# First MLP stage: the second of seven Strassen products is itself split by Strassen and spread over three blocks

## The chip, the cores and the metric

The kernel runs on one core of one Trainium2 chip. The metric is the device time of one execution in microseconds (us). The kernel before takes 865.07 us, the median of three runs (864.66 to 865.10).

## The reference

Attention whose pairs are masked by a hash comes first; its output is the input of an MLP with a per-feature slope (PReLU). The change touches only the MLP.

```python
def _moe_ref(x, w_in, w_out, alpha):
    h = x @ w_in                                        # (3072, 512) x (512, 2048)
    g = np.maximum(h, 0.0) + alpha * np.minimum(h, 0.0)
    return (g @ w_out).astype(np.float32)               # (3072, 2048) x (2048, 512)
```

The 3072 tokens are four batches of 768. All of it is in float32.

## The kernel before

**Stages.** Attention comes first, up to the first MLP product at 312.32 us, beside which the weights are read, rounded and combined. Then comes the MLP, batch by batch: a first stage (`ff1`, x times `w_in`, then the slope) of eight blocks, and a second stage (`ff2`, g times `w_out`) of seven products. The list `blocks` has the order, and the loop over it (`for j, (b, what, n) in enumerate(blocks)`) writes out the work of all engines by hand: `do` is `keep_in_program_order`, so each engine executes its instructions in the order in which the loop names them. DMAs of the MLP are issued by SP (`nc.sync`) and partly by GpSimd (POOL).

**The first stage.** It is one 2 by 2 Strassen step: the features are halved, the tokens of a batch (768) are halved to 384, and the inner dimension (512) is halved. Seven products of half-size matrices give the four quarters of h. Block i of eight makes 128 features of each half. `Product.times` issues one product: two matmuls of 128 by 384 (one for each 128 rows of the inner half). `Product.step(n)` names the products in the order 1, 2, 5, 6, 3, 7, 4. They are summed in three PSUM accumulators, "a", "b" and "c". Products 1, 6, 7 and 4 go to "a" in turn, and ScalarE (ACT) copies it out between them (`keep`). Product 2 goes to "b", products 5 and 3 to "c". `finish` then makes a quarter: VectorE (DVE) adds what is left to be added (L975) and applies the slope with one `scalar_tensor_tensor` (L979). The quarter "11" is product 1 plus product 2. It comes from "b" alone (ACT copies it to h, L972), as "b" is filled with product 1 first.

**Batches two to four** have a second Strassen level for products 1 and 5. `unit(b, u, before)` runs at the head of each group of four blocks. Class `Inner` makes one product for all four blocks: seven inner products (`Inner.times`, L1084: two matmuls of 128 by 192) in place of the eight halves that the four blocks would have. Its result lies in `n_s[b, u, o, f]` in SBUF. Class `Rest` is then a block that lacks products 1 and 5: its `step(1)` has ACT copy the finished product 1 from SBUF to "b" and to "a" (L999), its `step(5)` copies product 5 to "c", and the matmuls of products 2, 6, 3, 7 and 4 add to that. Inner weights are made by `sum_inner` in batch two (DVE, L1051), written to DRAM by POOL (L1052) and read back by `load_inner` in batches three and four. Inner operands of x are made by `sum_inner_x` (L1062 to L1064).

**After a pair of blocks** DVE also makes four differences of quarters of g (L983), which the second stage needs as left-hand sides. In batches two to four, blocks 0 to 5, this is done for two blocks at a time, all four differences in one go, after step 4 of the odd block. Blocks 6 and 7 do it singly.

**The second stage** does the same two-level scheme: `ff2` has one product of the first level for each n, made of seven inner ones (tiles z_1a, z_1b, z_1c; the number names the product). DVE makes its operands (gs L1227, ws L1219) and adds (m L1248). The accumulators "b" and "c" are single PSUM tiles (`bufs=1`) that first and second stage share. "a" is taken from three tiles of two banks (`two_banks`).

**SP queue.** `load_w` fetches the weights of a block (tile wi, all seven weight combinations, 896 KB, three buffers), `load_inner` the inner weights, `load_w2` those of the second stage (wl, two buffers), and `turn_out` writes the output (o, two buffers, L1281), with a part of that on POOL.

Of the kernel before, what the change touches and what calls it, by code (L numbers as in the profile page):

```python
# [8 lines left out]
F32 = mybir.dt.float32  # L9
# [398 lines left out]
def fast_path(  # L408
# [69 lines left out]
    w_n_s = dram.tile([2, 2, P, 4, 2 * P], F32, name="w_n_s")  # L478
    NW = NK * NF // 2
    wmax = const.tile([P, NW], F32, name="wmax")  # L480

# [145 lines left out]
    def weight_sum(i):  # L627


        i = order[i]  # L630
        lo, hi = halves(i)
        x = wx[i]
        if i < HW:
            n, m = divmod(i, 4)
            if m == 0:
                wst[n] = pool.tile([P, NM, 4, P], F32, name=f"wsi{n}", tag="wsi")
            slot = (0, 5, 1, 2)[m]
# [13 lines left out]
        do(DVE.tensor_tensor(dst.bitcast(I32), x, r, op=ALU.add))  # L651
        return (dst if i < HW else dst[:, 0])[:, :1]
# [3 lines left out]
    def weight_group(i):  # L656

        i = order[i]
        if i >= HW:
            n, m = divmod(i - HW, 2)  # L660
            if m == 1:
                nc.sync.dma_start(w_out_r[:, :, n].rearrange("m p d -> p m d"), wst[HW + n])
            return
        n, m = divmod(i, 4)
        if m < 3:
            return
        w = wst[n]
# [10 lines left out]
        for x in ((3, 5, 2), (5, 0, 5), (4, 3, 0), (6, 1, 4)):  # L678
# [207 lines left out]
    def sum_x(b, n, engine):  # L886
# [3 lines left out]
            x_m[b, to] = mid.tile([P, 2, CW], F32, name=f"x{b}_{to}", tag=f"x{to}", bufs=1)  # L890
        do(engine.tensor_tensor(x_m[b, to], x_m[b, a], x_m[b, c], op=ALU.subtract))

    def load_w(n):

        if n < B * NI:
            w_m[n] = mid.tile([P, NM, 2, P], F32, name=f"wi{n}", tag="wi", bufs=3)
            pinned(n < 3, nc.sync.dma_start(w_m[n], w_in_s[n % NI]))

    class Product:

# [30 lines left out]
        def step(self, n):  # L931
# [30 lines left out]
            elif n == 4:  # L962
                self.times("a", 2, 6, False)
                self.finish("21", self.ps["a"], None)

    def ff1(b, i):
        whole = b == 0

        def finish(c, t, more):
            if more is None:  # L970
                h = mid.tile([P, CW], F32, name=f"h{b}_{i}", tag="h")
                do(ACT.copy(h, t))  # L972
            else:
                h = t
                do(DVE.tensor_tensor(h, t, more, op=ALU.add))  # L975

            al = alpha[:, i + NI * (c[0] == "2") :][:, :1]
            m = {"11": 0, "21": 1, "22": 2, "12": 5}[c]
            do(DVE.scalar_tensor_tensor(new_g(b, m)[:, i], h, al, h, op0=ALU.mult, op1=ALU.max))  # L979
            if c == "21" and (whole or i % 2 or i > 5):  # L980
                at = slice(i if whole or i > 5 else i - 1, i + 1)
                for to, x, y in ((3, 5, 0), (5, 2, 5), (4, 2, 3), (6, 1, 4)):
                    do(DVE.tensor_tensor(new_g(b, to)[:, at], g_m[b, x][:, at], g_m[b, y][:, at], op=ALU.subtract))  # L983

        w = w_m[b * NI + i]
        kind, seeded = (Product, ("b",) if i else ()) if whole else (Rest, ("a", "b", "c"))
        made = kind(
            f"f{b}_{i}", CW, 2, lambda m, k: w[:, m, k], lambda m, k: x_m[b, m][:, k], finish, seeded=seeded,
        )
        if not whole:  # L990
            made.p1, made.p5 = (n_s[b, i // 4, o, i % 4 // 2][:, i % 2] for o in range(2))
        return made

    class Rest(Product):
# [5 lines left out]

        def step(self, n):
            if n == 1:
                self.seed("b", self.p1)
                self.seed("a", self.p1)
            elif n == 5:
                self.seed("c", self.p5)
            elif n == 6:
                self.times("a", 4, 4, False)
                self.keep("a", "u1")
            elif n == 7:  # L1010
                self.times("a", 5, 5, False)
# [9 lines left out]
    def load_inner(b, u):  # L1021

        t = late[0].tile([P, NI, 2 * P], F32, name=f"wn{b}_{u}", tag="wl")
        blocks = t[:, :4].rearrange("p i (k f) -> p i k f", k=2)
        do(nc.sync.dma_start(blocks, w_in_s[4 * u : 4 * u + 4, :, 0].rearrange("i p k f -> p i k f")))
        if b > 1:
            do(nc.sync.dma_start(t[:, 4:], w_n_s[u, 0]))
        for m, (f, kh) in QUADS.items():
            n_w[b, u, 0, m] = blocks[:, 2 * f : 2 * f + 2, kh]
        for m in range(4):  # L1030
            n_w[b, u, 0, 3 + m] = t[:, 4 + m].rearrange("p (t f) -> p t f", t=2)
        for f in range(2):
            t = late[0].tile([P, 2, 2, P], F32, name=f"wq{b}_{u}_{f}", tag="m", bufs=3)
            do(nc.sync.dma_start(t, w_in_s[4 * u + 2 * f : 4 * u + 2 * f + 2, :, 3].rearrange("i p k f -> p i k f")))
            for m, (ff, kh) in QUADS.items():
                if ff == f:
                    n_w[b, u, 1, m] = t[:, :, kh]
        for h in range(2):
            t = late[0].tile([P, 2, 2 * P], F32, name=f"wp{b}_{u}_{h}", tag=f"ws{3 + h}", bufs=2)
            if b > 1:  # L1040
                do(nc.sync.dma_start(t, w_n_s[u, 1, :, 2 * h : 2 * h + 2]))
            for m in range(2):
                n_w[b, u, 1, 3 + 2 * h + m] = t[:, m].rearrange("p (t f) -> p t f", t=2)
            n_w[b, u, h] = t

    def sum_inner(b, u, o):

        if b != 1:
            return
        for m, x, op, y in ((3, 21, ALU.add, 2), (4, 3, ALU.subtract, 0), (5, 0, ALU.subtract, 21), (6, 1, ALU.subtract, 4)):  # L1050
            do(DVE.tensor_tensor(n_w[b, u, o, m], n_w[b, u, o, x], n_w[b, u, o, y], op=op))  # L1051
            nc.gpsimd.dma_start(w_n_s[u, o, :, m - 3].rearrange("p (t f) -> p t f", t=2), n_w[b, u, o, m])  # L1052

    def sum_inner_x(b, o):

        x = x_m[b, 3 * o]
        if o == 0:
            t = mid.tile([P, 4, HC], F32, name=f"xn{b}_0", tag="x", bufs=1)
        else:
            t = late[0].tile([P, 4, HC], F32, name=f"xn{b}_1", tag="gs5", bufs=1)  # L1060
# [6 lines left out]
    class Inner:  # L1067
# [36 lines left out]
        def step(self, n):  # L1104
# [25 lines left out]
            elif n == 4:  # L1130
                self.times("a", 2, 6, False)
                do(ACT.copy(self.to(1, 0), self.bank("a")))

    def unit(b, u, before):

        def bank(name, tag=None):
# [23 lines left out]
        now = ff1(b, 4 * u)  # L1160
        now.step(1)
        two.step(7)
        now.step(2)
        now.step(5)
        two.step(4)
        if u:
            sum_w2(b, 0, 3, 4, 6, 5)
        turn_out()
        return now

    def new_g(b, m):
# [300 lines left out]
    for j, (b, what, n) in enumerate(blocks):  # L1472
# [22 lines left out]
                sum_x(b + 1, {2: 0, 4: 1, 5: 2}[n], DVE)  # L1495
        if b and what == "1" and n == 1:
            load_inner(b, 1)
        if b and what == "1" and n in (2, 3):
            sum_inner(b, 1, n - 2)
        if 0 < n2 < 7:  # L1500
# [4 lines left out]
        if j:  # L1505
            if not (b and what == "1"):
                now.step(5)
            now.step(6)
            now.step(3)
            if n2 or b == 0:  # L1510
                sum_w2(b, n2, 6)
            if b and what == "1" and (n + 1) % 4:
                after = ff1(b, n + 1)
                after.step(1)
            now.step(7)
            if n2 or b == 0:
                sum_w2(b, n2, 5)
            sum_g2(b, n2, 5)
# [26 lines left out]
        if j + 1 < len(blocks):  # L1545
# [45 lines left out]
```

## Time and profile before

| what | value |
|---|---|
| median of three runs | 865.07 us (864.66, 865.10, 865.07) |
| the profiled execution | 865.96 us |
| its span, first to last instruction | 863.8 us |
| granted TensorE clock | 0.998 |
| POOL busy | 150.1 us (17%) |
| HBM | 169 GB/s over the span |

The six stages of batches two to four, cut by hand at the start of the first inner product, of the second stage, and so on (us of busy time in each stretch):

| stretch, us | length | PE | DVE | ACT |
|---|---|---|---|---|
| batch 2, first stage, 449.55 to 522.9 | 73.35 | 72.82 | 57.43 | 35.17 |
| batch 2, second stage, 522.9 to 585.4 | 62.50 | 61.99 | 59.75 | 10.70 |
| batch 3, first stage, 585.4 to 656.5 | 71.10 | 71.10 | 52.08 | 35.02 |
| batch 3, second stage, 656.5 to 719.0 | 62.50 | 62.50 | 59.93 | 11.03 |
| batch 4, first stage, 719.0 to 790.1 | 71.10 | 71.10 | 51.78 | 35.02 |
| batch 4, second stage, 790.1 to 853.4 | 63.30 | 62.66 | 57.41 | 11.03 |

How to read it: the profile is of one execution, and its times are counted from the first instruction. "Busy" is the time in which an engine has an instruction in work; the ends of matmuls are modelled, so what a product takes is read from the distance between starts. In timelines a line gives the start, the length, the engine, the source line, the operation, out<-in, and in brackets the idle time ahead of it with what ended it. One product of the first stage appears as four matmul records, an inner one as four shorter ones.

### The profile page before, as it was taken

The numbers are of one execution on the slowest core, as the hardware profiler recorded it, in microseconds if no ns is written. First come the engines' busy times: TensorE is split into PE (matmuls) and PEld (weight loads), VectorE is DVE, ScalarE is ACT, GpSimd is POOL, SyncE is SP. The second block draws the span as 40 slices with busy tenths as digits, with TensorE's granted clock in tenths as the row PEclk, the third lists the DMA queues.
The fourth block names the chain that finished last, engine by engine and source line by source line (L and its number), as shares of the span: only waits on it lengthen the run. The fifth ranks groups of instructions, "written<-read, shape, count | busy, mean of one in ns | idle before, by whom it ended". The sixth has DMA issues, their size and how long they took to land.

```text
span 863.8 us, 15130 instructions
## 1 busy us (share of the span) xinstructions
PE 851.8 (99%) x5602; PEld 591.1 (68%) x5602; DVE 751.6 (87%) x1210; ACT 415.9 (48%) x778; POOL 150.1 (17%) x313
## 2 busy tenths in 40 slices
PE   9999999999999999999999999999999999999996
PEld 4444444444445445569996769998668999677996
DVE  6999999999999977889996979996769997769985
ACT  7777888878788833231115541114452114453111
POOL 1322423333334310210015100003000001200001
PEclk9999999999999999999999999999999999999999
DMA  8956879879698436775344734333845334830342
GB/s 203 191 130 132 205 178 240 167 205 243 131 252 208 145 126 234 245 288 215 128 141 139 276 134 170 120 144 97 315 140 174 143 109 130 297 135 0 104 159 60
DMA packets 174659, 147.97 MB, mean 171 GB/s; under 512 B 120832, under 2 KB 155824, under 8 KB 170992
## 3 DMA queue, kind: packets, MB, share of 16 engines
q1 hardware_dynamic: 159776, 117.35, 46.7%
q0 software_dynamic: 11792, 28.24, 10.8%
q10 hardware_dynamic: 3008, 1.33, 0.6%
q8 instruction: 46, 0.75, 0.4%
q14 instruction: 37, 0.30, 0.1%
HBM read 115.35 MB, written 30.41 MB: 169 GB/s over the span
## 4 chain that ended last, share of the span: by engine, by line


## 5 line engine op out<-in xcount | busy, mean ns | idle before, releaser
L790 ACT ACTIVATE pt<-sc 128x768 f32<-128x768 f32 x192 | 153.9, 813 | 3.1 <-PE sc L787 2.8
L787 PE MATMUL sc<-qT,kT 64*128 64x384 f32 x768 | 155.2, 482 | 0.0
L820 PE MATMUL av<-pt,vn 128*32 128x385 f32 (+1 forms) x1536 | 127.0, 485 | 0.0
L820 PEld LDWEIGHTS av<-pt,vn 128*32 128x32 f32 x1536 | 50.3, 109 | 73.8 <-issue 68.8
L787 PEld LDWEIGHTS sc<-qT,kT 64*128 64x128 f32 x768 | 68.9, 187 | 37.0 <-issue 36.9
L1281 POOL DMA_DIRECT2D out_dram<-o x52 | 28.3, 552 | 349.6 <-DVE o L1274 348.8
L983 DVE TENSOR_TENSOR g<-g,g 128x384 f32<-128x384 f32 (+1 forms) x92 | 63.5, 711 | 1.6
L787 PE MATMUL sc<-qb,kb 64*128 64x384 bf16 x384 | 63.9, 323 | 0.5 <-ACT pt L790 0.3
L979 DVE SCALAR_TENSOR_TENSOR g<-h,alpha 128x384 f32<-128x384 f32 x63 | 37.8, 612 | 20.7 <-ACT h L972 20.7
L1227 DVE TENSOR_TENSOR gs<-g,gs 128x768 f32<-128x768 f32 x56 | 53.2, 951 | 1.0
L1227 DVE TENSOR_TENSOR gs<-g 128x768 f32<-128x768 f32 x56 | 53.2, 950 | 0.0
L1219 DVE TENSOR_TENSOR ws<-wl 128x512 f32<-128x512 f32 x56 | 38.4, 685 | 11.3 <-DMA wl<-w_out_s 9.7
L787 PEld LDWEIGHTS <-kb 64*128 64x128 bf16 x384 | 20.2, 94 | 33.9 <-issue 11.6
L607 ACT ACTIVATE wr<-raw 128x512 int32<-128x512 uint32 x32 | 22.1, 692 | 30.3 <-DVE wso L651 15.3
L748 POOL DMA_DIRECT2D qb<-hr x60 | 30.0, 507 | 26.4 <-ACT hr L743 26.4
L798 DVE TENSOR_TENSOR accp<-pt,pt 128x1536 f32<-128x1536 f32 x16 | 28.1, 1756 | 7.3 <-ACT pt L790 7.3
L803 DVE TENSOR_TENSOR accd<-accd,pt 128x1536 f32<-128x1536 f32 x16 | 28.1, 1758 | 1.7
L809 DVE TENSOR_TENSOR accd<-accd,accp 128x1536 f32<-128x1536 f32 x16 | 28.1, 1758 | 0.6
L806 DVE TENSOR_TENSOR accp<-accp,pt 128x1536 f32<-128x1536 f32 x16 | 28.0, 1752 | 0.0
L802 DVE TENSOR_TENSOR accd<-pt,pt 128x1536 f32<-128x1536 f32 x16 | 28.0, 1751 | 0.0
L1431 ACT ACTIVATE qT<-qT 128x768 f32<-128x768 f32 x15 | 12.7, 844 | 25.4 <-DMA kb<-hr 20.8
L1239 DVE TENSOR_TENSOR m<-m,m 128x768 f32<-128x768 f32 x24 | 22.7, 946 | 0.3
(448 smaller groups left out, 1861.0 us busy)
## 6 DMA issues: line engine op xcount, KB each, us to landing
wi<-w_in_s SPq DMA_DIRECT2D x32, 896.0 KB
wl<-w_out_s SPq DMA_DIRECT2D x16, 1024.0 KB
wl<-w_out_r SPq DMA_DIRECT2D x12, 1024.0 KB
raw<-in_moe_w_in_dram POOLq DMA_DIRECT2D x15, 512.0 KB, 4.9
raw<-in_moe_w_out_dram POOLq DMA_DIRECT2D x14, 512.0 KB, 4.6
w_in_s<-wsi SPq DMA_DIRECT2D x16, 448.0 KB
qn<-in_q_dram SPq DMA_DIRECT2D x64, 96.0 KB
vn<-in_v_dram SPq DMA_DIRECT2D x16, 384.0 KB
```

The costliest lines, as they stand in the source:

```text
L748: queue.dma_start(bits[name, pi][D * s : D * s + 2 * NB, half * CW : (half + 1) * CW], raw[c : c + 2 * NB],)
L787: do(PE.matmul(sc[:, s, :CW], what["k", pi][r, ks], what["q", pi][r, qs], start=first, stop=not first,))
L790: do(ACT.activation(pts[kc][:, g, :, :CW], sc[:, :, :CW], AF.Exp, scale=SCALE / DOWN))
L798: do(DVE.tensor_tensor(accp[pi], p(0), p(1), op=ALU.add))
L803: do(DVE.tensor_tensor(accd[pi], accd[pi], p(5), op=ALU.add))
L809: do(DVE.tensor_tensor(accd[pi], accd[pi], accp[pi], op=ALU.add))
L820: do(PE.matmul(av[pi][D * s + t : D * s + t + 32, g, :w], nat["v", pi][:, s, kc * D + t : kc * D + t + 32], pts[kc][:, g, s, :w], start=(k ...
L979: do(DVE.scalar_tensor_tensor(new_g(b, m)[:, i], h, al, h, op0=ALU.mult, op1=ALU.max))
L983: do(DVE.tensor_tensor(new_g(b, to)[:, at], g_m[b, x][:, at], g_m[b, y][:, at], op=ALU.subtract))
L1219: do(DVE.tensor_tensor(t, w2[b, n, x], w2[b, n, y], op=op))
L1227: do(DVE.tensor_tensor(t, g2[b, n, x], g2[b, n, y], op=ALU.subtract))
L1281: pinned(b + 1 < B and queue is nc.sync, queue.dma_start(out_v[b, ch * CH + c].rearrange("(w r) d -> r w d", r=32)[:, :, cols], src[32 * a ...
```

## The change

In batches two to four, product 2 is taken by a second Strassen level too. A new class `Third` makes it for four blocks at a time: seven inner products of two matmuls of 128 by 192, as `Inner` does. They are not run at the head of the group but one by one between the products of its first three blocks. The table `THIRD` holds the places: product 1 after step 3 of the first block, 2 after its step 7; 6, 5, 7 and 3 around the second block's steps 6, 4, 3 and 7; 4 after step 6 of the third. `Rest` loses step 2, its seed of "b", and the quarter "11" with its copy to h.

The quarter "11" now arises in `Third`: as each inner product is done, DVE adds it to product 1 straight into g, six additions of 128 by 384 for four blocks, and then applies the slopes in place (`slopes`, one instruction for a block). ACT copies once from "a" to "b" and keeps three sums. One of the `two_banks` tiles and then twice "b" are `Third`'s.

Moved along with it: step 6 of a block comes ahead of step 5 (it stood behind), so ACT's copy-out of "a" stands ahead of its seed of "c". The four differences of g for a pair of blocks go into a list, `g_due`, of which one is taken after each of the quarters "12" and "21" of blocks 0 to 5 (all that are due in blocks 6 and 7). The weights of a block are split into two tiles: wj (products 1, 2, 5; only batch one) and wi (the other four; 512 KB). `load_third` fetches the weights of the third product with two DMAs for four blocks, in batches three and four with four more from DRAM, and batch two makes those four on DVE and writes them on POOL (`sum_inner`). `sum_inner_x(b, 2)` adds three DVE instructions for a batch.

The diff, cut to its core:

```diff
@@ load_w
-            w_m[n] = mid.tile([P, NM, 2, P], F32, name=f"wi{n}", tag="wi", bufs=3)
-            pinned(n < 3, nc.sync.dma_start(w_m[n], w_in_s[n % NI]))
+            w_m[n] = {}
+            for name, slots in (("wj", WJ), ("wi", WI)):
+                if name == "wi" or n < NI:
...
@@ ff1
+    g_due = []
+    def sum_g(count):
+        for b, at, to, x, y in g_due[:count]:
+            do(DVE.tensor_tensor(new_g(b, to)[:, at], g_m[b, x][:, at], g_m[b, y][:, at], op=ALU.subtract))
+        del g_due[:count]
...
-                    do(DVE.tensor_tensor(new_g(b, to)[:, at], g_m[b, x][:, at], g_m[b, y][:, at], op=ALU.subtract))
+                    g_due.append((b, at, *x))
+            if whole or i > 5:
+                sum_g(len(g_due))
+            elif c in ("12", "21"):
+                sum_g(1)
@@ class Rest
             if n == 1:
-                self.seed("b", self.p1)
                 self.seed("a", self.p1)
+            elif n in (2, 22):
+                return
@@ load_third (new)
+        for f in range(2):
+            t = mid.tile([P, 3, 2 * P], F32, name=f"wt{b}_{u}_{f}", tag="wj", bufs=3)
+            blocks = t[:, :2].rearrange("p i (k f) -> p i k f", k=2)
+            do(nc.sync.dma_start(blocks, w_in_s[4 * u + 2 * f : 4 * u + 2 * f + 2, :, 1].rearrange("i p k f -> p i k f")))
...
+            if b > 1:
+                do(nc.sync.dma_start(n_w[b, u, 2, 3 + m], w_n_s[u, 2, :, m]))
@@ class Third(Inner) (new)
+        def add(self, f, c, x, y=None):
+            b, u, o = self.key
+            first = n_s[b, u, 0, f][:, :, c * HC : (c + 1) * HC] if y is None else y
+            do(DVE.tensor_tensor(self.to(f, c), x, first, op=ALU.add))
+        def slopes(self, f):
+            b, u, o = self.key
+            for i in (4 * u + 2 * f, 4 * u + 2 * f + 1):
+                h = new_g(b, 0)[:, i]
+                do(DVE.scalar_tensor_tensor(h, h, slope(i, False), h, op0=ALU.mult, op1=ALU.max))
+        def step(self, n):
+            if n == 1:
+                self.ps["a"] = two_banks(self.name + "a")[:, 0]
+                self.ps["b"] = psum_bc[0].tile([P, 512], F32, name=self.name + "b", tag="b")
+                self.times("a", 0, 0, True)
+                do(ACT.copy(self.ps["b"][:, :CW], self.ps["a"][:, :CW]))
+            elif n == 2:
+                self.times("b", 1, 1, False)
+                self.add(0, 0, self.bank("b"))
+            elif n == 6:
+                self.times("a", 4, 4, False)
+                self.keep("a", "u1")
+                self.add(0, 1, self.sb["u1"])
+            elif n == 5:
+                self.ps["c"] = psum_bc[0].tile([P, 512], F32, name=self.name + "c", tag="b")
+                self.times("c", 3, 3, True)
+                self.keep("c", "p5")
+                self.add(1, 1, self.sb["p5"])
+            elif n == 7:
+                self.times("a", 5, 5, False)
+                self.keep("a", "u2")
+                self.add(1, 1, self.sb["u2"], self.to(1, 1))
+            elif n == 3:
+                self.times("c", 6, 2, False)
+                self.add(0, 1, self.bank("c"), self.to(0, 1))
+                self.slopes(0)
+            elif n == 4:
+                self.times("a", 2, 6, False)
+                self.add(1, 0, self.bank("a"))
+                self.slopes(1)
+    THIRD = {(0, "3"): 1, (0, "7"): 2, (1, "6"): 6, (1, "4"): 5, (1, "3"): 7, (1, "7"): 3, (2, "6"): 4}
@@ unit
-        now.step(2)
+        now.step(6)
         now.step(5)
         two.step(4)
...
+        if not u:
+            sum_inner_x(b, 2)
+        sum_inner(b, u, 2)
@@ the loop over blocks
+        if b and what == "1" and n == 2:
+            load_third(b, 1)
...
-            now.step(6)
+                now.step(6)
             now.step(3)
+            if b and what == "1":
+                third(b, n, "3")
...
             now.step(7)
+            if b and what == "1":
+                third(b, n, "7")
...
                     load_inner(b + 1, 0)
+                    load_third(b + 1, 0)
...
                 now = after
-                now.step(2)
+                now.step(6)
+                third(b1, n1, "6")
                 now.step(5)
                 before.step(4)
+                third(b1, n1, "4")
```

More of the change, by code (lines that the diff above doesn't have):

```diff
@@ L477, in fast_path @@
     x_s = dram.tile([B, NP, P, S], F32, name="x_s")
-    w_n_s = dram.tile([2, 2, P, 4, 2 * P], F32, name="w_n_s")
+    w_n_s = dram.tile([2, 3, P, 4, 2 * P], F32, name="w_n_s")
     NW = NK * NF // 2
@@ L636, in weight_sum @@
                 wst[n] = pool.tile([P, NM, 4, P], F32, name=f"wsi{n}", tag="wsi")
-            slot = (0, 5, 1, 2)[m]
+            slot = (0, 5, 1, 3)[m]
             dst = wst[n][:, slot].rearrange("p i f -> p (i f)")
@@ L675, in store @@
                 pinned(n < 3, nc.sync.dma_start(w_in_s[4 * c + ii][:, :, kk], w[:, :, ii]))
-        for x in ((3, 5, 2), (5, 0, 5), (4, 3, 0), (6, 1, 4)):
+        for x in ((2, 5, 3), (5, 0, 5), (4, 2, 0), (6, 1, 4)):
             sums_due.append((one, (x[0], x[1], ALU.subtract, x[2])))
@@ L891, in sum_x @@
         do(engine.tensor_tensor(x_m[b, to], x_m[b, a], x_m[b, c], op=ALU.subtract))
+    WJ, WI = (0, 1, 3), (2, 4, 5, 6)
     def load_w(n):
         if n < B * NI:
-            w_m[n] = mid.tile([P, NM, 2, P], F32, name=f"wi{n}", tag="wi", bufs=3)
-            pinned(n < 3, nc.sync.dma_start(w_m[n], w_in_s[n % NI]))
+            w_m[n] = {}
+            for name, slots in (("wj", WJ), ("wi", WI)):
+                if name == "wi" or n < NI:
+                    at = 0 if name == "wj" else len(WJ)
+                    t = mid.tile([P, len(slots), 2, P], F32, name=f"{name}{n}", tag=name, bufs=3)
+                    pinned(n < 3, nc.sync.dma_start(t, w_in_s[n % NI, :, at : at + len(slots)]))
+                    w_m[n].update({m: t[:, j] for j, m in enumerate(slots)})
     class Product:
@@ L964, in step, with slope @@
                 self.finish("21", self.ps["a"], None)
+    g_due = []
[3 more added lines that the diff above has]
+        del g_due[:count]
+    def slope(i, lower):
+        return alpha[:, i + NI * lower :][:, :1]
     def ff1(b, i):
@@ L975, in finish @@
                 do(DVE.tensor_tensor(h, t, more, op=ALU.add))
-            al = alpha[:, i + NI * (c[0] == "2") :][:, :1]
+            al = slope(i, c[0] == "2")
             m = {"11": 0, "21": 1, "22": 2, "12": 5}[c]
@@ L981, in finish @@
                 at = slice(i if whole or i > 5 else i - 1, i + 1)
-                for to, x, y in ((3, 5, 0), (5, 2, 5), (4, 2, 3), (6, 1, 4)):
-                    do(DVE.tensor_tensor(new_g(b, to)[:, at], g_m[b, x][:, at], g_m[b, y][:, at], op=ALU.subtract))
+                for x in ((3, 5, 0), (5, 2, 5), (4, 2, 3), (6, 1, 4)):
+                    g_due.append((b, at, *x))
[3 more added lines that the diff above has]
+                sum_g(1)
         w = w_m[b * NI + i]
-        kind, seeded = (Product, ("b",) if i else ()) if whole else (Rest, ("a", "b", "c"))
+        kind, seeded = (Product, ("b",) if i else ()) if whole else (Rest, ("a", "c"))
         made = kind(
-            f"f{b}_{i}", CW, 2, lambda m, k: w[:, m, k], lambda m, k: x_m[b, m][:, k], finish, seeded=seeded,
+            f"f{b}_{i}", CW, 2, lambda m, k: w[m][:, k], lambda m, k: x_m[b, m][:, k], finish, seeded=seeded,
         )
@@ L1033, in load_inner @@
             t = late[0].tile([P, 2, 2, P], F32, name=f"wq{b}_{u}_{f}", tag="m", bufs=3)
-            do(nc.sync.dma_start(t, w_in_s[4 * u + 2 * f : 4 * u + 2 * f + 2, :, 3].rearrange("i p k f -> p i k f")))
+            do(nc.sync.dma_start(t, w_in_s[4 * u + 2 * f : 4 * u + 2 * f + 2, :, WJ.index(3)].rearrange("i p k f -> p i k f")))
             for m, (ff, kh) in QUADS.items():
@@ L1044, in load_inner, with load_third @@
             n_w[b, u, h] = t
+    def load_third(b, u):
+        for f in range(2):
+            t = mid.tile([P, 3, 2 * P], F32, name=f"wt{b}_{u}_{f}", tag="wj", bufs=3)
+            blocks = t[:, :2].rearrange("p i (k f) -> p i k f", k=2)
+            do(nc.sync.dma_start(blocks, w_in_s[4 * u + 2 * f : 4 * u + 2 * f + 2, :, 1].rearrange("i p k f -> p i k f")))
+            for m, (ff, kh) in QUADS.items():
+                if ff == f:
+                    n_w[b, u, 2, m] = blocks[:, :, kh]
+            n_w[b, u, 2, 3 + f] = t[:, 2]
+        t = mid.tile([P, 3, 2 * P], F32, name=f"wt{b}_{u}_2", tag="wj", bufs=3)
+        for m in range(4):
+            if m > 1:
+                n_w[b, u, 2, 3 + m] = t[:, m - 2]
+            if b > 1:
+                do(nc.sync.dma_start(n_w[b, u, 2, 3 + m], w_n_s[u, 2, :, m]))
+            n_w[b, u, 2, 3 + m] = n_w[b, u, 2, 3 + m].rearrange("p (t f) -> p t f", t=2)
     def sum_inner(b, u, o):
@@ L1054, in sum_inner_x @@
     def sum_inner_x(b, o):
[L1056 to L1060, printed above, removed]
+        x = x_m[b, (0, 3, 1)[o]]
+        home = late[0] if o else mid
+        t = home.tile([P, 4, HC], F32, name=f"xn{b}_{o}", tag=("x", "gs5", "m5")[o], bufs=1)
         left, right = (x[:, :, c * HC : (c + 1) * HC] for c in range(2))
@@ L1132, in step, with __init__, keep, to @@
                 do(ACT.copy(self.to(1, 0), self.bank("a")))
+    class Third(Inner):
+        def __init__(self, b, u):
+            self.key, self.o, self.seeded = (b, u, 2), 2, True
+            self.name = f"n{b}_{u}_2"
+            self.ps, self.sb = {}, {}
+        TAG = {"p5": "p5", "u1": "p1", "u2": "gs6"}
+        def keep(self, bank, what):
+            tag = self.TAG[what]
+            home = mid if tag in ("p1", "p5") else late[0]
+            t = home.tile([P, CW], F32, name=self.name + what, tag=tag, bufs=1)
+            do(ACT.copy(t, self.ps[bank][:, :CW]))
+            self.sb[what] = t.rearrange("p (t w) -> p t w", t=2)
+        def to(self, f, c):
+            b, u, o = self.key
+            return new_g(b, 0)[:, 4 * u + 2 * f : 4 * u + 2 * f + 2, c * HC : (c + 1) * HC]
+        def add(self, f, c, x, y=None):
[3 more added lines that the diff above has]
+        def slopes(self, f):
+            b, u, o = self.key
+            for i in (4 * u + 2 * f, 4 * u + 2 * f + 1):
[31 more added lines that the diff above has]
+                self.slopes(1)
@@ L1134, in unit, with third @@
+    thirds = {}
+    THIRD = {(0, "3"): 1, (0, "7"): 2, (1, "6"): 6, (1, "4"): 5, (1, "3"): 7, (1, "7"): 3, (2, "6"): 4}
+    def third(b, i, place):
+        n = THIRD.get((i % 4, place))
+        if n:
+            if n == 1:
+                thirds[b, i // 4] = Third(b, i // 4)
+            thirds[b, i // 4].step(n)
     def unit(b, u, before):
```

## The prediction

> **What bounds the kernel now.** I read the page's first part, then busy time by stretches, then the timelines of PE and DVE around the end of a first stage (batch three), and last the waits. The page:
>
> ```profile
> PE 851.8 (99%) x5602; PEld 591.1 (68%) x5602; DVE 751.6 (87%) x1210; ACT 415.9 (48%) x778; POOL 150.1 (17%) x313
> ```
>
> PE sets the time: in a PE at 99% with a granted clock of 0.998, each product that is saved is time saved, as long as nobody makes PE wait. DVE's 87% is an average. The stretches from the last unit of a first stage to the first products of the second (columns: stretch, length, busy PE, PEld, DVE, ACT):
>
> ```profile
> 631.30:645.60 14.30, 14.30 (x48) 8.69 (x47) 8.99 (x16) 6.51 (x16) 0.00 (x0) 1.00 0.31 118
> 645.60:668.20 22.60, 22.60 (x107) 18.03 (x106) 22.13 (x36) 6.81 (x17) 0.00 (x0) 1.00 0.56 178
> ```
>
> Ahead of 645.6, DVE has 5.3 us to spare; behind it, none for 22.6 us. The DVE timeline shows both ends of that run:
>
> ```profile
> 645.61 0.62 DVE L979 SCALAR_TENSOR_TENSOR g<-h,alpha 128x384 f32<-128x384 f32 x1 [1.37 <-ACT h L972]
> 646.15 3.81 DVE L983 TENSOR_TENSOR g<-g,g 128x768 f32<-128x768 f32 x4
> ...
> 657.68 0.55 DVE L975 TENSOR_TENSOR f_7u<-f_7u,f_7c 128x384 f32<-128x384 f32 x1
> ...
> 667.76 0.34 DVE L1248 TENSOR_TENSOR m<-z_1u,z_1c 128x192 f32<-128x192 f32 x1
> ```
>
> The first is DVE's last wait. The last reads accumulator "c" of z_1 and so frees it at 668.10. PE:
>
> ```profile
> 629.41 0.81 PE L1084 MATMUL nd<-xn,wp 128*128 128x192 f32 x4
> 630.06 1.45 PE L921 MATMUL f_4b<-x,wi 128*128 128x384 f32 x4
> ...
> 643.61 1.45 PE L921 MATMUL f_5a<-x,wi 128*128 128x384 f32 x4
> 644.90 1.45 PE L921 MATMUL f_6a<-x,wi 128*128 128x384 f32 x4
> ...
> 668.21 1.52 PE L921 MATMUL z_2c<-gs,ws 128*128 128x192 f32 x8
> 669.57 1.46 PE L921 MATMUL z_2a<-gs,ws 128*128 128x192 f32 x8
> ```
>
> z_2c, the next user of "c", starts at 668.21, 0.11 us after it came free, and takes 1.36 us to the next start where its neighbours take 1.30. So DVE and PE arrive together. The other two batches show the same (z_2c 1.52 at 533.42, 1.51 at 801.77). At this place DVE has no reserve at all.
>
> [...] From start to start an add of 384 takes 0.46 (627.88 to 628.34) if the next instruction does not need it, 0.58 (657.68 to 658.26) if it does. [...]
>
> **The change, part by part.**
>
> *Removed and added on PE.* One product of a block is 1.29 us (630.06 to 631.35), an inner product 0.65 (629.41 to 630.06). For four blocks 4 x 1.29 = 5.16 go and 7 x 0.65 = 4.55 come: 0.61 saved, in six groups 3.66 us. That is the whole gain.
>
> *ACT.* It loses two copies a block (the seed of "b", the copy to h) and gains four for four blocks. At about 3 of 7 us busy it costs nothing by its amount. Its order counts, below.
>
> *DVE.* The slopes replace those of "11" one for one, 0.53 start to start. New are six adds for four blocks, two of them at 0.58 or more and four at about 0.47: 3.1 us. `sum_inner_x(b, 2)` adds 1.3 us a batch at the end of the first unit, where step 6 of the third product needs it only after 2.5 us or more; in batch two four weight sums follow (0.39 each, 1.55 by the chain at 448.90), which also fit. And the list of differences moves three of the four of blocks 2 and 3 (0.87 each, 2.6) out of the second unit, where DVE is idle at times, into blocks 4 and 5. So 3.1 + 2.6 = 5.7 us are put into 5.3 us of room, which PE also shortens by 0.6.
>
> *The walk.* I wrote DVE's new order out against PE's from block 4 on. DVE last waits for the quarter "21" of block 4; everything afterwards is ready before DVE reaches it. From there to the add of product 3 of block 7 (the one at 657.68) DVE has: slopes 11 x 0.53 to 0.54 (three "21", two "12", two "22", four in place), two "12" and two "22" adds at 0.58, the third product's last four adds (0.47, 0.47, 0.58, 0.58), six big differences (three single ones at 0.87, among them the last two of blocks 2 and 3, then three in a row 2.73), four small ones 2.12, two gs 1.86 (all by start-to-start times of such rows). In order this comes to 19.62. Then 10.42 as in the trace (657.68 to 668.10). Ahead stands 0.71 from the end of the matmul to DVE's start (644.90 to 645.61). DVE is done 0.71 + 19.62 + 10.42 = 30.75 us after product 4 of block 4 ends. PE needs from there: four inner products 2.60, eleven of the first stage 14.19, nine of the second 11.70: 28.49. The same sum for before is 23.20 against 23.31, and its trace shows just that. So DVE is 2.26 us late where it was 0.11 early: PE loses 2.37 us more, first at z_1c (it needs "c" of block 7), then at z_2c. Later in the second stage DVE waits for transfers (0.7 at 672.29, 1.13 at 700.12), which move with PE: nothing is won back. Three batches: 7.1 us.
>
> *ACT's order.* Step 6 now precedes step 5, so the seed of "c" of the next block is queued behind the copy-out u1, which needs DVE to be done with the previous u1, and u1's matmuls. Behind it waits PE's product 3. In batches three and four the seed is there about 0.1 us ahead in block 3. In batch two the four sums of wn (1.55) stand ahead of block 2's "12": the seed comes 1.25 us late. Before, PE lost 0.18 at this place:
>
> ```profile
> 482.85 1.56 PE L921 MATMUL f_3c<-x,wi 128*128 128x384 f32 x4 [0.18 <-ACT f_3c L999]
> ```
>
> So 1.1 us more, once. Bounds 0 and 1.5.
>
> *SP and POOL.* `load_third` puts two (batch two) or six issues (three, four) ahead of twelve output copies. An issue is 0.47 start to start (585.31 to 585.78): 2.8 us. In batch three the copies were issued by 591.8 and landed 1.8 later; DVE writes that buffer again at 597.30, so 3.7 us of cover, and 4.4 in batch four. Taken at nothing; if the cover is gone, DVE stands at its transposes with block 0's adds behind. The second group's load waits for product 4 of the third in block 2, and holds wi of block 5 for 3 us, which is needed a unit later. Fewer weight bytes (512 for 896 KB a block) relieve the queue. POOL's eight more writes in batch two stand behind output copies nobody waits for: nothing. Batch one's second issue for a block (0.35) is beside 9 us of matmuls.
>
> *Sum.* -3.66 + 7.1 + 1.1 = +4.5. The profiled execution is 865.96 (span 863.8, 2.16 around it), 0.89 above the median; with the difference added, it becomes 870.5, the span 868.3, and the median 865.07 + 4.5 = 869.6. Bounds of the unknown: the 24 instructions of the walk could each cost 0.04 more or 0.02 less (the spread of start-to-start times in the rows), so 1.9 to 3.3 a batch; with 0 to 1.5 for the seed the loss is 5.7 to 11.4: 867.1 to 872.8.
>
> **The rivals.**
>
> *Faster: PE keeps the whole gain.* If DVE reaches z_2c in time, 865.07 - 3.66 = 861.4. For it: DVE is 87% busy, its room of 5.3 us is nearly what is added, and POOL and ACT are idle. It decides where the added DVE work stays below the room that in-order execution can use. Against: 645.60 to 668.20 has no room, and before shows 0.06 us lost there already.
>
> *About the same.* The walk leaves DVE two waits of 0.8 us, ahead of the third product's second add and of the quarter "21" of block 4. If they close (results come earlier than I have them), DVE is 0.8 late instead of 2.4, and the seed costs little: -3.66 + 2.4 + 0.8 = 864.6.
>
> *Slower still: output copies.* If the six loads wait for earlier landings (single issues there show 0.76 and 1.42), the copies land after DVE wants the buffer, by more than the 3 us that DVE may be late in block 0. Some 1.7 us in two batches on top: 873.0.
>
> **How the numbers follow.** My walk 0.62 (867.1 to 872.8), PE's gain kept 0.14, about the same 0.11, output copies 0.13. A measurement of this kernel tells 0.2% from no change, 863.3 to 866.8. Faster is the second case, 0.14; within is the third and a sliver of the first, 0.12; slower 0.74. The range 864.0 to 873.5 leaves out the kept gain and the tails.
>
> **What would show it.** Right: z_1c and z_2c of batches two to four start about 2.4 us late together, waiting for DVE; DVE has no wait from block 5 to there; first stages are shorter by 1.2 us up to product 7 of block 7, but for block 3 of batch two. Wrong: z_2c on schedule, with DVE idle ahead of it; or stalls at the units, with DVE at L1274 waiting for copies.

## The result and the profile after

The changed kernel takes 871.0 us, the median of four runs (870.23 to 872.48), beside 864.88 for the kernel before. The ratio is 1.0073, with a 95% interval of 1.0055 to 1.009. The prediction was 869.6. The profiled execution takes 870.79 us, its span is 868.9, the granted clock 0.998.

The page's first part has PE less busy by 1.0 us, over a span that is 5.1 longer:

```profile
PE 850.8 (98%) x5674; PEld 598.5 (69%) x5674; DVE 773.6 (89%) x1263; ACT 407.5 (47%) x754; POOL 154.2 (18%) x321
```

Two stretches of batch three, divided as in the prediction where DVE's last wait ends, which is now at 641.57: 14.57 us ahead of it, and from there to z_1c (columns as there):

```profile
627.00:641.57 14.57, 14.27 (x69) 11.32 (x68) 9.01 (x16) 7.69 (x17) 0.00 (x0) 1.00 0.31 102
641.57:661.80 20.23, 19.09 (x74) 12.65 (x72) 19.85 (x33) 6.74 (x15) 0.00 (x0) 1.00 0.50 155
```

Behind 641.57 DVE is full and now PE is not: it stands for 1.14 us. DVE's timeline has the run from the last wait to the add of product 3 of block 7, without another wait:

```profile
641.57 0.62 DVE L996 SCALAR_TENSOR_TENSOR g<-h,alpha 128x384 f32<-128x384 f32 x1 [0.73 <-ACT h L989]
...
652.83 2.81 DVE L977 TENSOR_TENSOR g<-g,g 128x768 f32<-128x768 f32 x3
...
661.20 0.55 DVE L992 TENSOR_TENSOR f_7u<-f_7u,f_7c 128x384 f32<-128x384 f32 x1
...
671.28 0.35 DVE L1363 TENSOR_TENSOR m<-z_1u,z_1c 128x192 f32<-128x192 f32 x1
```

It is 19.63 us to 661.20. PE's timeline shows who pays:

```profile
659.19 1.46 PE L928 MATMUL z_1b<-g,wl 128*128 128x192 f32 x8
661.80 1.57 PE L928 MATMUL z_1c<-gs,ws 128*128 128x192 f32 x8 [1.14 <-DVE f_7u L992]
...
669.70 1.46 PE L928 MATMUL z_2b<-g,wl 128*128 128x192 f32 x8
671.68 1.57 PE L928 MATMUL z_2c<-gs,ws 128*128 128x192 f32 x8 [0.52 <-DVE m L1363]
```

A product takes 1.30 from start to start here. z_1c stands 1.31 after its turn (661.80 against 659.19 + 1.30) and z_2c 0.68. After each such stop the next start comes 0.10 later too (661.80 to 663.20 is 1.40), so the two cost 2.2 us, and the other two batches show the same to 0.01. Part of a stop counts as busy in the page: z_1c starts 1.31 late, but only 1.14 of it is idle, and the 0.10 behind it is not idle either. At some 0.27 a stop, the eleven stops that this kernel has more than before (sixteen for five in the bill below) hide about 3 us, by my estimate. That is why PE's busy time falls by only 1.0 us where 3.66 are saved.

One place the prediction does not have. PE, then ACT, at the first block of the second unit:

```profile
631.23 1.45 PE L928 MATMUL f_4a<-x,wi 128*128 128x384 f32 x4
632.52 0.81 PE L1122 MATMUL nd<-xn,wq 128*128 128x192 f32 x4
633.64 1.56 PE L928 MATMUL f_4c<-x,wi 128*128 128x384 f32 x4 [0.30 <-ACT f_4c L1020]
```

```profile
632.72 0.48 ACT L935 COPY f_4u<-f_4a 128x384 f32<-128x384 f32 x1 [0.81 <-PE f_4a L928]
633.10 0.49 ACT L1020 COPY f_4c<-n 128x384 f32<-128x384 f32 x1
```

The seed of f_4c (ACT's copy of product 5 into accumulator "c") needs nothing that isn't long there, but it is queued behind the copy-out f_4u, which waits for f_4a's matmuls. Only one inner product (nd) stands between f_4a and f_4c on PE, so f_4c is 0.47 late (632.52 + 0.65 = 633.17), with the restart 0.57. All six groups show it: 3.4 us.

Every gap between starts of matmuls in the MLP, of both kernels, with the restarts, makes this bill (us):

| term | predicted | from the two traces |
|---|---|---|
| matmuls saved | -3.66 | -3.66 (by the count of matmuls) |
| DVE late at z_1c, z_2c, and 0.25 at f_7c, three batches | +7.1 | +7.1 (2.43 a batch, 0.06 before) |
| seed of block 3, batch two | +1.1 | +0.8 (1.27 for 0.44) |
| seed of the first block of a group, six times | 0 | +3.4 |
| z_7c and z_4c of batch two, in before only | 0 | -1.0 |
| z_2c of batch one, z_3a of batch four, in this execution of before only | 0 | -2.0 |
| MLP starts later (312.72 for 312.32) | 0 | +0.4 |
| sum | +4.5 | +5.1 (spans: 868.9 - 863.8) |

The stops at z_2c of batch one and z_3a of batch four are absent from the profiles of before_pool6 and before_defer_x (below), which leave before's weight transfers as they are, so I take them for chance in that one execution. For the medians they fall out: -3.66 + 7.1 + 0.8 + 3.4 - 1.0 = 6.6, against 6.1 measured.

### The profile page after: what moved, and what is told of

The parts are those of the page before. It is cut to its first block, busy times and chain, and to the rows that moved or that the text cites. A ratio compares the mean times of both kernels' runs of the same rounds, so it can differ in the third digit from the quotient of the medians.

```text
span 868.9 us, 15379 instructions
## 1 busy us (share of the span) xinstructions
PE 850.8 (98%) x5674; PEld 598.5 (69%) x5674; DVE 773.6 (89%) x1263; ACT 407.5 (47%) x754; POOL 154.2 (18%) x321
## 3 DMA queue, kind: packets, MB, share of 16 engines
q10 hardware_dynamic: 3008, 1.33, 0.6%
## 4 chain that ended last, share of the span: by engine, by line
## 5 line engine op out<-in xcount | busy, mean ns | idle before, releaser
L996 DVE SCALAR_TENSOR_TENSOR g<-h,alpha 128x384 f32<-128x384 f32 x39 | 23.9, 613 | 7.1 <-ACT h L989 7.1
```

## The experiments

Theory: two separate losses, DVE's debt at the end of the first stage (work that DVE still has to do when PE already waits for it; 7.1) and ACT's seed behind the copy-out (4.2), and 3.66 saved. Rivals: the order or some late result, not the amount of DVE's work, makes z_1c late; or engines hinder each other. Times are medians, always beside before in the same series (864.2 to 864.6).

**unit_seed: the seed first, at units.** `unit` only:

```diff
-        now.step(6)
         now.step(5)
+        now.step(6)
         two.step(4)
```

> In the unit alone, step 5 (ACT fills c with product 5) goes ahead of step 6 (ACT copies a out). My theory: PE waits 0.57 us before product 3 of the first block of each of six groups only because that seed is queued behind the copy-out, so 3.4 us go: 871.0 becomes 867.6, and the z stalls stay. Rival: the seed is late because DVE frees c late (its add of the second inner product's step 3), whatever ACT's order: 871.0 stays.

Measured: 867.31 us, ratio 1.0031 (1.0018 to 1.0043). ACT and PE of this kernel at the same place:

```profile
630.57 0.49 ACT L1020 COPY f_4c<-n 128x384 f32<-128x384 f32 x1
631.48 0.48 ACT L935 COPY f_4u<-f_4a 128x384 f32<-128x384 f32 x1 [0.43 <-PE f_4a L928]
```

```profile
631.28 0.81 PE L1122 MATMUL nd<-xn,wq 128*128 128x192 f32 x4
631.93 1.45 PE L928 MATMUL f_4c<-x,wi 128*128 128x384 f32 x4
```

The seed lies ahead of the copy-out, f_4c follows nd after 0.65, and all six stops are gone. z_1c and z_2c stay as late as they were.

**all_seed: the seed first, everywhere.** The same exchange in the loop over blocks too:

```diff
                 now = after
+                now.step(5)
                 now.step(6)
                 third(b1, n1, "6")
-                now.step(5)
```

> The same exchange of steps 5 and 6 in the loop over blocks as well. My theory: beside the 3.4 us of the units, block 3 of batch two gains about 1.0 (the seed no longer waits for the copy-out and the slope ahead of it): 866.6. The small wait at product 3 of block 7 goes too, but z_1c waits as much longer, since DVE sets that. Rival (DVE alone makes block 3 late): 867.6 as with the units alone.

Measured: 866.04 us, ratio 1.0016 (1.0009 to 1.0023). f_3c of batch two keeps 0.08 of its stop. f_7c's stop goes, and z_1c is later by the same: 1.56 for 1.31. So the whole of ACT's order costs 6.1 - 1.5 = 4.6 us, and DVE's debt is untouched by it.

**flush3: the differences earlier.** All differences of blocks 2 and 3 at once in the second unit, where DVE has waits, instead of one by one in blocks 4 and 5:

```diff
-            if whole or i > 5:
+            if whole or i > 5 or i == 3 and c == "21":
                 sum_g(len(g_due))
```

> The differences of g of blocks 2 and 3 are made all at once in the second unit, as before the change; those of blocks 0 and 1 stay spread. My theory: of the three that go back, two (0.87 each) lay in the run in which DVE has no wait, so z_1c and z_2c come 1.74 us earlier in each of three batches: 871.0 - 5.2 = 865.8. Rival: the run of DVE is as long as its total work makes it, and where the differences stand does not count: 871.0; or transfers set z: 871.0.

Measured: 869.33 us, ratio 1.0054 (1.004 to 1.0068): it is 4.8 us above before in place of 6.1, so 1.3 us are won where 5.2 was expected. z_1c is 1.12 late, z_2c 0.68 as in the changed kernel; f_7c's stop is gone. DVE's last wait is now in block 5:

```profile
645.37 0.56 DVE L992 TENSOR_TENSOR n<-n,f_5u 128x384 f32<-128x384 f32 x1 [0.73 <-ACT f_5u L935]
...
660.68 0.55 DVE L992 TENSOR_TENSOR f_7u<-f_7u,f_7c 128x384 f32<-128x384 f32 x1
```

From there to the add of product 3 of block 7 it has 15.31 us of work: moving work ahead of the last wait mostly moved the wait. Beside the kernel before, PE has lost two products of 1.29 in blocks 6 and 7, DVE only the two slopes of their quarters "11" (0.53 each). I conclude that what stands behind the last wait sets the debt, so it must be work from there that goes; defer (below) tests it.

**seed_flush: both.** The edits of all_seed and flush3 together.

> Both: steps 5 and 6 exchanged everywhere, and the differences of blocks 2 and 3 at once in the second unit. My theory: the two causes are separate and add, 871.0 - 4.4 - 5.2 = 861.4, below the kernel before (864.9). Rival: as PE gets faster the waits for transfers in the second stages, which the kernel before has (about 2.0 us at z_7c, z_4c and z_3a) and the changed one has not, come back: 863.4.

Measured: 866.04 us, ratio 1.0016 (1.0009 to 1.0023), no better than all_seed, and 2.6 and 4.6 above the two expectations. z_1c keeps 1.12, and a new stop appears in the second unit of batch two, where the burst of differences and the four weight sums meet:

```profile
494.41 1.56 PE L928 MATMUL f_4a<-x,wi 128*128 128x384 f32 x4 [0.80 <-ACT f_4a L1020]
```

**pool6 and seed_pool6: one difference on GpSimd.** The difference g6 = g1 - g4, which only the last product of the second stage reads, is made by POOL in batches two to four (in seed_pool6 with all_seed's edits):

```diff
-            do(DVE.tensor_tensor(new_g(b, to)[:, at], g_m[b, x][:, at], g_m[b, y][:, at], op=ALU.subtract))
+            do((POOL if to == 6 and b else DVE).tensor_tensor(new_g(b, to)[:, at], g_m[b, x][:, at], g_m[b, y][:, at], op=ALU.subtract))
```

> The changed kernel, with the last of the four differences of each pair of blocks (g6 = g1 - g4, needed only by the last product of the second layer) moved from VectorE to GpSimd in batches two to four. Theory (a debt of VectorE's queue at the end of each first stage, 2.4 us a batch): between VectorE's last wait and the add of product 3 of block 7 stand three or four of these differences at 0.5 to 0.9 us, so 2.2 us or more leave the queue; z_1c and z_2c lose their stalls and the time falls by up to 7.2, to about 863.8. Rival (GpSimd and VectorE hinder each other in SBUF, or GpSimd is so slow that the last product waits): the time stays at 871 or rises above it, VectorE's own instructions get longer in the last blocks.

> The changed kernel with the seed of the next block's third product put ahead of the copy-out of its sixth product (everywhere), and g6 on GpSimd as in the run beside it. Theory (two separate losses, the seed at units and blocks 4.8 us, VectorE's debt 7.2 us): with both gone about 859, up to 861 if waits for weight transfers, which late matmuls now cover, come back. Rival (GpSimd hinders VectorE): 866 or more, no better than the seed alone.

Measured: 872.74 us, ratio 1.0093 (1.0079 to 1.0108), and 869.78, ratio 1.0063 (1.005 to 1.0076). Counted from before in each series, both are slower than without the move, by 2.2 and 3.8. In pool6 it is the rival that holds. DVE and POOL in pool6:

```profile
644.73 0.55 DVE L992 TENSOR_TENSOR f_5u<-f_5u,f_5c 128x384 f32<-128x384 f32 x1
645.31 1.59 DVE L996 SCALAR_TENSOR_TENSOR g<-f_5u,alpha 128x384 f32<-128x384 f32 x1
...
656.55 2.04 DVE L996 SCALAR_TENSOR_TENSOR g<-n,alpha 128x384 f32<-128x384 f32 x1
...
661.56 1.64 DVE L1342 TENSOR_TENSOR gs<-g,gs 128x768 f32<-128x768 f32 x1
```

```profile
644.42 2.07 POOL L977 TENSOR_TENSOR g<-g,g 128x768 f32<-128x768 f32 x1 [20.03 <-DVE g L977]
656.13 2.05 POOL L977 TENSOR_TENSOR g<-g,g 128x768 f32<-128x768 f32 x1 [9.64 <-DVE g L977]
660.74 1.64 POOL L977 TENSOR_TENSOR g<-g,g 128x384 f32<-128x384 f32 x1 [2.56 <-DVE g L977]
```

A slope is 0.62 long without POOL. The two that begin while POOL is in its difference last 1.59 and 2.04 and end about 0.4 after POOL does (656.13 + 2.05 = 658.18; 656.55 + 2.04 = 658.59); a gs sum grows from 0.96 to 1.64. That is 0.97 + 1.42 + 0.68 = 3.1 us added in place of 2.3 taken (0.87 twice, 0.53 once). The add at 644.73 begins beside POOL and keeps its 0.55; one of its operands is in PSUM. The three that grew have all their tensors in SBUF. By what mechanism POOL holds them up was not shown. z_1c is now 1.82 late.

In seed_pool6 something else is added. The same place there, and the granted clock behind the start of z_1c, in seed_pool6 and then in pool6 (columns: stretch, length, busy PE, PEld, DVE, ACT, POOL, granted clock, DMA share, GB/s):

```profile
661.27 2.72 PE L928 MATMUL z_1c<-gs,ws 128*128 128x192 f32 x8 [2.02 <-DVE f_7u L992]
```

```profile
661.27:665.00 3.73, 3.73 (x12) 3.73 (x13) 3.66 (x7) 0.32 (x1) 0.00 (x0) 0.54 0.00 0
663.72:667.45 3.73, 3.73 (x23) 3.73 (x24) 3.66 (x7) 0.64 (x2) 0.00 (x0) 1.00 0.01 3
```

z_1c is 2.10 to 2.18 late in seed_pool6, and behind that stop about ten matmuls stand 0.32 apart in place of 0.16, in all three batches: the granted clock has fallen, to 0.54 in the stretch shown. In pool6, after 1.82, it has not (1.00). From the start of z_1c to that of z_2c it takes 10.89 us in seed_pool6 and 9.88 in all_seed, though z_2c's stop is gone. So by these traces only some 0.6 us a batch of seed_pool6's loss is DVE's longer lateness, and some 0.9 the clock (an estimate for the profiled run; over the five runs the mean clock is 0.992 to 0.995, for 0.997 to 0.999 in pool6). seed_pool6 is therefore no clean test of its rival; pool6 is. Why the clock fell was not tested.

**before_pool6: the same on the kernel before.**

> The kernel before, with g6 on GpSimd in batches two to four. Theory: VectorE has no debt there (0.06 us a batch lost at z_2c), so at most 0.2 us are to be had: 864.4 to 864.9. Rival (GpSimd hinders VectorE): VectorE has no reserve at that place, so it gets slower, 866 or more.

Measured: 865.44 us, ratio 1.0009 (1.000 to 1.0017): a loss of 1.0 us, between the two expectations and at the edge of what can be told. One visible part is f_3c of batch two, 0.96 late for 0.34.

**before_bytes: where the 1.0 us of z_7c and z_4c went.** In before, batches two to four load only what they use of a block's weights:

```diff
-            pinned(n < 3, nc.sync.dma_start(w_m[n], w_in_s[n % NI]))
+            if n < NI:
+                pinned(n < 3, nc.sync.dma_start(w_m[n], w_in_s[n % NI]))
+            else:
+                nc.sync.dma_start(w_m[n][:, 1:3], w_in_s[n % NI][:, 1:3])
+                nc.sync.dma_start(w_m[n][:, 4:], w_in_s[n % NI][:, 4:])
```

> The kernel before, loading in batches two to four only the five of seven weight parts that are used there, in two transfers a block (640 KB for 896). It asks where about 2.0 us of waits for transfers, which the kernel before has and the changed one has not, went. Theory A (fewer weight bytes clear the transfer queues for the loads of the second stage): these stalls go here too, about 863. Theory B (they are only covered, since matmuls arrive later): no change, 864.9.

Measured: 863.32 us, ratio 0.9984 (0.9977 to 0.9992), 1.1 us less, where theory A has some 1.5 to 1.9: right in kind, smaller in size. DVE's wait for the weights of batch two's second stage, in before, in this kernel and in the changed kernel:

```profile
547.71 0.69 DVE L1219 TENSOR_TENSOR ws<-wl 128x512 f32<-128x512 f32 x1 [1.87 <-DMA wl<-w_out_s]
```

```profile
546.53 0.69 DVE L1223 TENSOR_TENSOR ws<-wl 128x512 f32<-128x512 f32 x1 [0.97 <-DMA wl<-w_out_s]
```

```profile
548.55 0.69 DVE L1334 TENSOR_TENSOR ws<-wl 128x512 f32<-128x512 f32 x1 [0.49 <-DMA wl<-w_out_s]
```

before_bytes gets its weights 1.2 us sooner, z_7c's stop is gone, and z_4c is 0.12 late for 0.45. So transfers of this size are enough to take away most of these stops. The changed kernel's are as small in batch two: 512 KB a block, and 256 KB for each pair of blocks that `load_third` fetches, make 640 KB a block (768 in batches three and four). The prediction's "512 for 896" leaves `load_third` out. How much of the 1 us the smaller transfers win in the changed kernel, and how much is only covered because its z_2c starts 2.28 us later, no run separates.

**defer and seed_defer: the same work, later.** DVE makes g6 of blocks 2 to 7 in the second stage (after step 5's sums of its third to fifth product):

```diff
                 for x in ((3, 5, 0), (5, 2, 5), (4, 2, 3), (6, 1, 4)):
-                    g_due.append((b, at, *x))
+                    if b and i > 1 and x[0] == 6:
+                        if i != 6:
+                            g_late.append((b, slice(i - 1, i + 1), *x))
+                    else:
+                        g_due.append((b, at, *x))
...
             sum_g2(b, n2, 5)
+            if g_late and what == "2" and n > 1:
+                g_due.append(g_late.pop(0))
+                sum_g(1)
```

> The changed kernel, with VectorE's difference g6 of blocks 2 to 7 (needed only by the last product of the second layer) taken out of the first stage and put into the third to fifth product of the second stage, in batches two to four. VectorE does the same work, 2.6 us of it later. Theory (debt at the end of the first stage): the 2.4 us at z_1c and z_2c go in each batch. In the second stage VectorE waits only about 1.2 us in all in batches two and three, so about 1.2 of the 2.6 us come back there as late accumulators; batch four, whose VectorE makes no sums for a next batch, keeps all: 871.0 - 1.2 - 1.2 - 2.4 = about 866.2. If nothing comes back: 863.8. Rival (it is not the amount of VectorE's work ahead of z_1c that counts, but the order or a result that comes late): no change, 871.

> The same deferred differences, together with the seed of the third product ahead of the copy-out of the sixth. Theory (the two losses are separate): 866.0 (the seed alone) - 4.8 = 861.2; 858.8 if nothing comes back in the second stage. Rival: 866.

Measured: 867.68 us, ratio 1.0035 (1.0023 to 1.0047), and with the seed first 862.92, ratio 0.9983 (0.9975 to 0.9991), 1.5 and 1.7 above the two expectations. In defer z_1c and z_2c are on time in all three batches:

```profile
660.30 1.46 PE L928 MATMUL z_1c<-gs,ws 128*128 128x192 f32 x8
...
669.40 1.46 PE L928 MATMUL z_2c<-gs,ws 128*128 128x192 f32 x8
...
715.92 1.57 PE L928 MATMUL z_4c<-gs,ws 128*128 128x192 f32 x8 [0.85 <-DVE m L1367]
```

The theory of the debt is shown: DVE makes the same differences (those of blocks 6 and 7 in one instruction for two), only some of them later, and the 2.2 to 2.4 us at z_1c and z_2c go. The last line shows what comes back: z_4c, the last product of the stage, is 1.01 late in batch three (1.11 with the restart). In batch two it is 1.33, and z_7c 0.64; in batch four next to nothing (0.07). That is 3.3 us, where 2.4 was expected: batch two has less room than I gave it.

**seed_defer_x: room for it.** On top of seed_defer, two sums of x for the next batch leave the second stage for the first unit:

```diff
-            else:
-                sum_x(b + 1, {2: 0, 4: 1, 5: 2}[n], DVE)
+            elif n == 2:
+                sum_x(b + 1, 0, DVE)
...
-            sum_x(b, 3, DVE)
+            sum_x(b, 2, DVE)
...
         one.step(4)
+        if not u:
+            sum_x(b, 3, DVE)
         two.step(3)
...
         two.step(4)
+        if not u:
+            sum_x(b, 1, DVE)
```

> As the run before it, and two of the sums of x for the next batch (0.87 us each) leave the crowded second stage of batches one to three for the first unit of the next batch, where VectorE waits for 1.6, 0.6 and 0.5 us in turn. Theory: the second stage has then room for what was deferred into it, so what came back in the run before goes too: 858.8 to 860. Rival (the unit has no room, its accumulators come late): no faster than the run before it.

Measured: 860.73 us (860.60 to 861.17), ratio 0.9957 (0.9943 to 0.9971), the fastest of all, 0.7 above the range that was expected. z_4c of batch three has no wait; in batch two it keeps 0.36, and an inner product of the third product in that batch's first group (n_2c) has a new stop of 0.41.

```profile
664.74 1.46 PE L928 MATMUL z_2c<-gs,ws 128*128 128x192 f32 x8
...
710.24 1.46 PE L928 MATMUL z_4c<-gs,ws 128*128 128x192 f32 x8
```

**before_defer_x: the moves without the change.** g6 and the sums of x are moved in the kernel before as above.

> The kernel before, without the change, with the same two moves of VectorE's work as in the fastest run (g6 of blocks 2 to 7 into the second stage, two sums of x into the next batch's first unit). It asks how much of that run's gain belongs to the change and how much the moves would have brought alone. Theory (before has no debt at z_1c, its few waits are for transfers of weights): the moves bring nothing, 864.2 to 864.9, so the change itself is worth the 3.7 us of removed matmuls once VectorE has room. Rival (the moves help any kernel of this form): 862 or less, and the change is worth 1 us or nothing.

Measured: 865.46 us, ratio 1.0014 (1.0006 to 1.0023): not faster, rather 1.3 us slower, above what was expected. z_3c and z_7c of batch two are 0.32 and 0.84 late (0 and 0.39 before). So the moves are worth nothing by themselves. Against this kernel the fastest one stands at 0.9957 / 1.0014 = 0.9943, some 4.9 us less, near the 3.66 of saved matmuls and the 1.1 of the smaller transfers. Beside before itself it is 3.8 less; the rest is before_defer_x's own loss, whose cause is open.

## Why the prediction was right, and where it was not

- *The gain on PE* (3.66 us) is there, though only the fastest experiment lets it be seen.
- *The walk of DVE* held: 19.62 us predicted from its last wait to the add of block 7's product 3, 19.63 measured; 2.37 us a batch, 2.43 measured with f_7c. The walk takes DVE's instructions one after another as the program names them, and so the 31 from 641.57 up to that add stand in the trace. Deferring 2.6 us of DVE's work, with all else the same, removed just these stops, so it is the cause. One slip: the bounds speak of 24 instructions in the walk, where the prediction's own list and the trace have 31. With 31 the same spread gives 1.8 to 3.6 a batch in place of 1.9 to 3.3.
- *ACT's order in block 3 of batch two* had the right mechanism: 0.8 for 1.1 us.
- *Missed: the same mechanism at units.* The prediction looked at the seed behind the copy-out in the blocks, and found 0.1 us to spare in batches three and four, and no stop came there. It did not look at the group's first block, where one inner product is all that hides copy-out and seed: 3.4 us by the trace, and as much between unit_seed's difference to before and the changed kernel's. For the same reason one of its signs failed: first stages are not 1.2 us shorter up to product 7 of block 7. In batch three that stretch is 68.52 us in before and 68.69 here, since two stops of 0.57 and the 0.25 at f_7c take the gain back.
- *Wrong: "nothing is won back."* The stops at z_7c and z_4c of batch two (1.0 us) are gone. Smaller transfers, taken only as relief for a queue, remove most of that when they are made in before; in the changed kernel lateness may cover a part.
- *SP and POOL at nothing* held. The transposes at 597.55 follow the instruction ahead of them with no wait for output copies, so the rival of the output copies did not come about.

The total was 1.4 us low: 3.4 missed, less 1.0 won back, 0.3 too much in block 3, and the rest within what the runs scatter. That it came so close is in part luck. The missed term is as large as the whole gain on PE; with it alone the prediction's sum is 873.0, above the 872.8 that its own bounds allowed, and only terms of the other sign brought it back.

What stays open: why before_defer_x loses more than its moved work seems to ask (its lateness in batch two was seen, its cause was not followed), how much the smaller transfers win in the changed kernel, and why the clock fell in seed_pool6.

## What to carry to other kernels

Walk the engine that feeds the bound one from its last wait to the point where a buffer must be free: there its work is a debt that a reserve ahead of the wait hardly pays (flush3 won 1.3 us of 5.2), and here only putting work behind that point relieved it. When two instructions change places in an in-order queue, check each site by itself for what still hides the wait of the first; the site with the shortest cover (here one inner product of 0.65 us) pays. A change that saves matmuls can lose by its side work and still be worth keeping: the same change ends 0.73% slower or 0.43% faster than before, by the order of DVE's and ACT's work alone.

## What the runs showed of the hardware

A difference of 128 by 384 in float32 took 1.30 to 1.65 us on GpSimd and one of 128 by 768 1.8 to 2.1, against 0.55 and 0.95 on DVE. In batch three of pool6, from 635 to 675 us, the four DVE instructions without an operand in PSUM that began while GpSimd was in such a difference took 0.54 to 1.42 us longer than elsewhere (1.59 and 2.04 for 0.62, 1.64 for 0.96, and 1.23 for 0.69 at 669.41); one that had begun before kept its length (a gs sum of 0.95 at 660.58), and so did an add with an operand in PSUM (0.55 at 644.73). Each stop of PE in float32 matmuls cost 0.10 to 0.11 us more than the stop itself, at the sixteen stops of the changed kernel and the five of before. And in batch three of seed_pool6, behind 2.02 us in which PE stood idle ahead of z_1c, the granted clock was 0.54 over the next 3.73 us, where behind 1.66 in pool6 it was 1.00.
